# Moving the wait for the output store from SyncE into the gathering instruction of the closing barrier

## The chip, the cores and the metric

The kernel runs on one core of a Trainium2 chip. Its time is the device time of one execution in microseconds, and a run gives one such time, with a trace of the same execution. The span is the time between the first and the last record of the program in the trace; the timed execution is some 1.8 us longer than the span (1271.76 against 1270.0 us for the profiled execution before), and in the trace no instruction has a record in those 1.8 us.

The store is called "landed" when its semaphore takes its last step, and its "flight" is the time from its issue until then. In this document "tail" means: from the last step of the output store's semaphore to the end of the span. It is read from the trace's own records, which are in ns; the views print tenths of a microsecond.

## The reference

Attention over a cache for one new token, mixed with a small dense block by a gate. Cut to what matters:

```python
def reference(A_x, A_k_cache, A_v_cache, A_wq, A_wo, B_x, B_w1, B_b1, B_w2, B_b2, gate_w):
    g = _sigmoid((A_x * gate_w).sum(-1, keepdims=True))
    a = _A_ref(A_x, A_k_cache, A_v_cache, A_wq, A_wo)   # caches: 2 x 8 x 32768 x 256, bf16
    b = _B_ref(B_x, B_w1, B_b1, B_w2, B_b2)             # 448 -> 1792 -> 448
    return g * a + (1 - g) * b                          # out: 2 x 1 x 448
```

The two caches are almost all of the 547 MB that are read. The output is two rows of 448 bf16 values, 1.8 KB.

## The kernel before

Each engine has its own program inside one block. SyncE issues the loads and, at the end, the store. VectorE and ScalarE each write half of the output tile and step the semaphore `mix`; SyncE waits for both, issues the store and waits until it has landed.

```python
        def prog_sp(E):
            ...                                    # all loads
            E.wait_total("mix")
            dma(lambda e: e.dma_start(out[:, 0, :], out_sb), "d_out", "out")
            E.wait_total("d_out")                  # the store has landed
        ...
        with nc.Block("main") as block:
            ...
            block.gpsimd(lambda eng: run("pool", eng))
            block.sync(lambda eng: run("sp", eng))
            block.tensor(lambda eng: run("pe", eng))
            block.scalar(lambda eng: run("act", eng))
            block.vector(lambda eng: run("dve", eng))
```

The block closes with a barrier over the five engines: each of four reports to GpSimd, which gathers the reports and then releases all. `gather` and `release` are the two semaphores of that barrier. In the program as it is built, each engine first branches into a last block, which holds:

```text
ScalarE, TensorE, VectorE, SyncE, each:   Drain            wait: release = 0, update: gather + 1   (the report)
                                          EventSemaphore   wait: release >= 1, update: release - 1     (the take)
GpSimd:                                   Drain
                                          EventSemaphore   wait: gather >= 4, update: gather - 4       (the gather)
                                          EventSemaphore   update: release + 4                         (the release)
```

The semaphores stand on these instructions in the trace's records too; in the kernel before, `gather` takes its four steps 24, 382, 441 and 1752 ns after the start of the last cast, and the gather starts at 1776.

A wait is written as an instruction of its own, and the built program can carry it on the instruction that follows: in the trace SyncE's wait for the store stands on its branch into the last block, a record of 33 ns that starts 16 ns after the store's last step.

## Time and profile before

| | before |
|---|---|
| timed, median of the first 3 runs | 1271.65 us (1271.5 to 1271.76) |
| span of the profiled execution | 1270.0 us |
| last cast ends | 1268.38 us |
| store: issue starts, issue ends, semaphore's last step | 1268.403, 1268.732, 1269.558 us |
| tail | 1269.955 - 1269.558 = 0.397 us |

Read it from the top: the bulk is the loading of the caches (431 GB/s over the span, the DMA engines 90% busy or more in 39 of 40 slices), and no part of the change touches it. What the change can move is in the last line. The prediction shows the lines of each view.

### The profile page before, as it was taken

Reading aid. Unit: us, or ns where it says so; the run is one execution under the profiler, and the core shown is the slowest. Engines: PE = TensorE matmul, PEld = TensorE weight load, DVE = VectorE, ACT = ScalarE, POOL = GpSimd, SP = SyncE. Lnnn points to the kernel's source line nnn. Section 1 sums busy time; section 2 is a strip of 40 time slices with the busy share of each in tenths; the row PEclk is TensorE's granted clock in tenths of the full one; section 3 lists DMA queues with packets and bytes.
Section 4 is the critical chain, followed back from the end, with each engine's and each line's share of the span. In section 5 each row is a group of like instructions: output and inputs, shape, how many; then the busy total and the mean of one; then the engine's idle time right before and its main releaser. Section 6 shows DMA issues by size and latency. Waiting matters only on the chain.

```text
span 1270.0 us, 7459 instructions
## 1 busy us (share of the span) xinstructions
PE 698.5 (55%) x4386; PEld 140.6 (11%) x1842; DVE 689.9 (54%) x311; ACT 44.8 (4%) x184; POOL 4.4 (0%) x19
## 2 busy tenths in 40 slices
PE   0976456644466454565545666444764446655455
PEld 0211011100011110111001111000110001111012
DVE  4575536655365563556735466453665636557351
ACT  0100000000000000000000000000000000000000
POOL 1000000000000000000000000000000000000000
PEclk9877788777788777877768887678877778877787
DMA  9999999999999999999999999999999999999998
GB/s 408 450 429 430 430 431 436 442 431 430 429 431 438 431 438 438 431 431 429 431 438 431 436 440 431 429 431 431 440 429 436 440 431 429 431 431 440 429 425 369
DMA packets 11114, 547.58 MB, mean 431 GB/s; under 512 B 1368, under 2 KB 1632, under 8 KB 2144
## 3 DMA queue, kind: packets, MB, share of 16 engines
q1 hardware_dynamic: 10948, 547.43, 99.7%
q8 instruction: 7, 0.11, 0.0%
q10 hardware_dynamic: 156, 0.01, 0.0%
q14 instruction: 3, 0.02, 0.0%
HBM read 547.43 MB, written 0.00 MB: 431 GB/s over the span
## 4 chain that ended last, share of the span: by engine, by line
DMA 58%; PE 20%; DVE 15%; issue 5%; another core or an unknown queue 2%; ACT 0%; ACTq 0%; SPq 0%; DVEq 0%
DMA ring<-in_A_k_cache_dram 54%; DVE ring L760 12%; PE ps_s L527 7%; PE ps_s L342 6%; PE ps_o L342 4%; DMA ring<-in_A_v_cache_dram 3%; PE ps_o L576 1%; DMA PT<-in_gate_w_dram 1%; DVE mx L764 1%; PE ps_m L541 0%; PE ps_m L536 0%; PE ps_f L588 0%; DVE gmax L766 0%; PE ps_o L470 0%
## 5 line engine op out<-in xcount | busy, mean ns | idle before, releaser
L760 DVE STREAM_TRANSPOSE ring<-ring 128x4096 uint32<-128x4096 uint32 x128 | 557.6, 4413 | 385.0 <-DMA ring<-in_A_k_cache_dram 384.7
L527 PE MATMUL ps_s<-ring,Abd 128*128 128x512 bf16 x1024 | 427.9, 418 | 399.7 <-DVE ring L760 399.2
L342 PE MATMUL ps_s<-ring,Abd 128*128 128x512 bf16 x1024 | 424.4, 414 | 0.0
L527 PEld LDWEIGHTS ps_s<-ring,Abd 128*128 128x128 bf16 x1024 | 106.2, 104 | 822.1 <-DVE ring L760 456.6
L342 PE MATMUL ps_o<-ring,PT 128*24 128x512 bf16 x1504 | 112.0, 405 | 0.0
L546 PE MATMUL ps_f<-o_sb,selg 128*32 128x257 f32 x32 | 17.0, 635 | 91.1 <-DVE o_sb L793 89.9
L576 PE MATMUL ps_o<-ring,PT 128*24 128x512 bf16 x544 | 56.6, 415 | 14.3 <-DMA ring<-in_A_v_cache_dram 14.3
L764 DVE TENSOR_REDUCE mx<-ps_s 128x1 f32<-128x1024 f32 x16 | 19.6, 1225 | 60.8 <-PE ps_s L342 60.8
L677 ACT ACTIVATE negm<-ps_m 128x1 f32<-128x1 f32 x16 | 2.7, 171 | 1133.7 <-PE ps_m L541 1133.7
L777 DVE STREAM_TRANSPOSE PT<-pexp 128x1024 bf16<-128x1024 bf16 x16 | 19.9, 1245 | 36.7 <-PE ps_o L342 36.7
L793 DVE TENSOR_REDUCE o_sb<-ps_o 128x256 f32<-128x2048 f32 x15 | 34.4, 2291 | 0.5
L791 DVE TENSOR_TENSOR ps_o<-ps_o,mask 128x2048 f32<-128x2048 f32 x15 | 34.3, 2290 | 0.0
L576 PEld LDWEIGHTS ps_o<-ring,PT 128*24 128x24 bf16 x544 | 14.5, 98 | 103.9 <-issue 85.2
L774 DVE COPY ls<-lsum 128x1 f32<-128x1 f32 x16 | 2.5, 154 | 32.0 <-ACT pexp L681 32.0
L671 ACT COPY Abd<-qrep 32x16 bf16 (+1 forms) x128 | 19.5, 199 | 0.6
L681 ACT ACTIVATE pexp<-ps_s,negm 128x1024 bf16<-128x1024 f32 x16 | 17.8, 1114 | 1.7
L536 PE MATMUL ps_m<-ident_f,mx 128*1 128x128 f32 x32 | 6.1, 271 | 21.1 <-DVE mx L764 21.1
L441 PE MATMUL ps_o<-ring,xT 128*32 128x512 bf16 x16 | 5.0, 501 | 20.4 <-issue 20.4
L546 PEld LDWEIGHTS ps_f<-o_sb,selg 128*32 128x32 f32 x32 | 2.9, 140 | 109.2 <-DVE o_sb L793 107.1
L541 PE MATMUL ps_m<-ones_f,gmx 1*128 1x1 f32 x32 | 6.3, 262 | 9.9 <-DVE gmx L770 9.9
L807 DVE TENSOR_SCALAR o_sb<-ps_o,mask 128x256 f32<-128x256 f32 x1 | 0.5, 484 | 17.0 <-PE ps_o L342 17.0
L766 DVE TENSOR_REDUCE gmax<-ps_m 1x2 f32<-1x128 f32 x16 | 4.5, 278 | 7.5 <-PE ps_m L536 7.5
(87 smaller groups left out, 75.3 us busy)
## 6 DMA issues: line engine op xcount, KB each, us to landing
ring<-in_A_v_cache_dram SPq DMA_DIRECT2D x1, 4096.0 KB, 27.2
ring<-in_A_v_cache_dram SPq DMA_DIRECT2D x2, 2048.0 KB, 34.0
ring<-in_A_wq_dram SPq DMA_DIRECT2D x1, 3072.0 KB, 28.5
ring<-in_B_w_dram SPq DMA_DIRECT2D x1, 1568.0 KB, 34.5
ring<-in_A_wo_dram SPq DMA_DIRECT2D x1, 1568.0 KB, 37.9
ring<-in_B_w_dram SPq DMA_DIRECT2D x1, 1344.0 KB, 32.2
ring<-in_A_wo_dram SPq DMA_DIRECT2D x1, 1008.0 KB, 39.8
ring<-in_A_wo_dram SPq DMA_DIRECT2D x1, 560.0 KB, 40.7
```

The source lines that it names most:

```text
L342: return e.add_instruction(mybir.InstMatmult(name=f"I-{nc.next_id()}", engine=mybir.EngineType.PE, ldweights=False, ins=[e.lower_ap(x), e. ...
L527: fn = lambda e, o=o, x=x, st=st, sp=sp, s=s, w=w: e.matmul(o, a_win(s, w), x, start=st, stop=sp, skip_group_check=True)
L541: E.ins(lambda e: e.matmul(ps_m[:, C_BC:C_BC + 1], gmx[:, :], ones_f[0:1, 0:1], start=True, stop=True), key=("M2", g))
L546: E.ins(lambda e: e.matmul(ps_oa, selg[:, :], o_sb[:, :], start=False, stop=False, skip_group_check=True), key=("OT", g))
L576: fn = lambda e, o=o, x=x, wt=wt, st=st, sp=sp, j=j: e.matmul(o, wt, x, start=st, stop=sp, skip_group_check=True)
L671: E.ins(lambda e, o=o, Q=Q, c=c: e.copy(o[:, :, c:c + 2], qrep[32 * Q:32 * Q + 32, :, bass.ds(E.dyn(2 * g, 2), 2)]), key=(("A", g) if (Q = ...
L681: E.ins(lambda e: e.activation(pexp[:, :].rearrange("p (r i a) -> p i r a", r=CR, i=2), ps_s[:, :].rearrange("p (i r a) -> p i r a", i=2, ...
L760: E.ins(lambda e: e.transpose(k_words(idx, blk), k_words(idx, blk)), key=("T", idx, blk))
L764: E.ins(lambda e: e.tensor_reduce(mx[:, :], ps_s[:, :], AX.X, ALU.max), key=("MX", g))
L777: E.ins(lambda e: e.transpose(PT[:, :], pexp[:, :]), key=("PT", g))
L791: E.ins(lambda e: e.tensor_tensor(p, p, mb, ALU.mult), key=("OM", g))
L793: E.ins(lambda e: e.tensor_reduce(o_sb[:, 0:Dh], ps_o[:, :].rearrange("p (n d) -> p d n", d=Dh), AX.X, ALU.add), key=("OS", g))
```

## The change

The intent: SyncE walks through its branch and its drain, and reports to the barrier, while the store is still under way; only the gather waits for the store.

```diff
             E.wait_total("mix")
             dma(lambda e: e.dma_start(out[:, 0, :], out_sb), "d_out", "out")
-            E.wait_total("d_out")
-
         def prog_pe(E):
...
             block.vector(lambda eng: run("dve", eng))
 
 
+        done = nc.main_func.blocks[-1]
+        n0 = len(done.instructions)
+        engs["pool"].eng = nc.gpsimd
+        engs["pool"].wait_total("d_out")
+        ins = done.instructions
+        at = next(i for i, x in enumerate(ins) if x.engine == mybir.EngineType.Pool and type(x).__name__ == "InstEventSemaphore")
+        done.instructions = ins[:at] + ins[n0:] + ins[at:n0]
```

The added lines append GpSimd's wait to the last block and move it directly ahead of the gather.

## The prediction

About 0.19 us off, 1271.65 - 0.19 = 1271.46, put down as 1271.45 us.

> **What bounds the kernel now.** I read the page from the whole to the end: first the slices, then the chain that ended last, then the timeline of the last two microseconds, then the wait lists of SyncE and the view of the line that closes the block, because the change touches nothing ahead of the last store. The first view says what the bulk of the time is.
>
> ```profile
> span 1270.0 us, 7459 instructions
> ...
> DMA  9999999999999999999999999999999999999998
> ...
> HBM read 547.43 MB, written 0.00 MB: 431 GB/s over the span
> ```
>
> The 16 DMA engines are 90% busy or more in 39 of 40 slices and read the two caches at 431 GB/s. The bulk is set by what is loaded, and no load, buffer or release of a buffer is in the diff. So only the tail after the last load can change. The chain of waits, asked for its last stretch, and the timeline show it.
>
> ```profile
> 1263.41 4.57 PE ps_f L588 x62
> 1267.97 0.02 issue
> 1268.00 0.38 DVE pexp L846
> ```
>
> ```profile
> 1268.00 0.34 ACT L697 CAST pexp<-ps_f 2x224 bf16<-2x224 f32 x1 [45.80 <-PE ps_f L588]
> 1268.00 0.38 DVE L846 CAST pexp<-ps_f 2x224 bf16<-2x224 f32 x1 [7.03 <-PE ps_f L588]
> 1268.40 0.33 SPq L413 DMA_DIRECT2D out_dram<-pexp  x1
> ```
>
> The columns are start and length in us. The reader is to see that the chain view stops at the last cast (1268.00 + 0.38 = 1268.38), 1.6 us ahead of the end of the span: the store and the closing barrier are sequencer work, which it doesn't show. They are in SyncE's wait list (us in total, times, longest) and in the view of the block's last line (duration in ns, then first and last start in us).
>
> ```profile
> SPq L866 <- DMA out_dram<-pexp: 0.8, 1, 0.8
> ...
> SPq L866 <- PEq L866: 0.2, 1, 0.2
> ```
>
> ```profile
> L866 POOLq EVENT_SEMAPHORE  x2: 17/17/17, 1269.8 to 1269.8; - x2
> L866 POOLq DRAIN  x1: 529/529/529, 4.8 to 4.8; - x1
> L866 PEldq DRAIN  x1: 437/437/437, 1267.6 to 1267.6; - x1
> L866 ACTq DRAIN  x1: 368/368/368, 1268.0 to 1268.0; - x1
> L866 DVEq DRAIN  x1: 418/418/418, 1268.0 to 1268.0; - x1
> L866 SPq COMPARE_BRANCH  x1: 33/33/33, 1269.6 to 1269.6; - x1
> L866 SPq DRAIN  x1: 7/7/7, 1269.7 to 1269.7; - x1
> L866 SPq EVENT_SEMAPHORE  x1: 17/17/17, 1269.9 to 1269.9; - x1
> ```
>
> The views round to 0.1 us, so I took the same records from the trace itself, in ns after 1269 us: the store's semaphore takes its last step at 558; SyncE's branch, on which the compiled program put the wait for the store, starts at 574; SyncE's drain, which reports to the barrier, at 739; GpSimd's gather, which waits for four reports, at 772; GpSimd's release at 850; SyncE, ScalarE, VectorE and TensorE take the release at 892 to 904, and the last ends at 955, which is the end of the span. The other three reported long before: their drains end at 1268.01 (TensorE), 1268.37 (ScalarE) and 1268.43 us (VectorE). So SyncE is the last to arrive, and it arrives late because it waits for the store first and walks through a branch and a drain afterwards.
>
> [...] the branch lasts 33 ns though SyncE stood 0.8 us before it, and its start lies 16 ns after the semaphore's last step. [...] three steps, at 1268.845, 1269.526 and 1269.558 us, for a store of two rows; a waiter on GpSimd has to wait for the third just as SyncE does. [...] Here the store takes 1269.558 - 1268.403 = 1.155 us from the start of its issue to its last step, 0.826 us of it after the issue has ended (1268.732)[...].
>
> **The change part by part.**
> - Removed: SyncE's wait for the store ahead of its branch. It is no instruction of its own in this trace, so none disappears. What it did was to hold the branch until 1269.574 us.
> - Moved: SyncE's branch and drain. They start right after the issue. From the wait's end, the drain started 739 - 574 = 165 ns after the branch, and the gather 33 ns after the drain. With the issue ending at 1268.732, I expect the branch near 1268.75, the drain near 1268.92 and the report visible near 1268.95 us. That is some 0.6 us before the store lands, all of it under the store's flight.
> - Added: the wait for the store, on GpSimd. It is placed directly before the gather. In this trace two pure waits in a row on TensorE appear as one EVENT_SEMAPHORE with two wait terms (three such records, 51 ns each, like its single ones), so I expect GpSimd's gather to become one instruction with two waits, still 17 ns long, rather than a new instruction. I choose that as the main case; the other is a rival below.
> - The new end: the gather now waits for the store alone, since four reports are in by 1268.95. After a DMA's last step SyncE took 16 ns to start; by the trace's records VectorE took 23 to 24 ns in every one of its waits that ended with a cache tile's last landing, and TensorE 28 to 29 ns in those where a sequencer instruction waited. I take 16 to 28 ns for GpSimd, so the gather starts at 558 + 16 to 558 + 28 = 574 to 586 instead of 772: earlier by 186 to 198 ns. Everything after it (78 ns to the release, 42 to 54 ns to the four takers, 51 ns for the last) stays.
> - Sum: about 0.19 us off a span of 1270.0 us, which is 0.015%. On the timed median: 1271.65 - 0.19 = 1271.46, predicted as 1271.45 us.
>
> **The rivals.**
> 1. The wait stays an instruction of its own on GpSimd. Then it starts at about 580, and the gather follows one step later. The only pair of semaphore instructions in a row on GpSimd here is gather and release, 78 ns apart at both barriers (607 and 686 ns after the start of the span; 772 and 850 at the end). The gain shrinks to 772 - (580 + 78) = 0.11 us: 1271.54 us. The word "in" of the change's description speaks against it, as do TensorE's double waits.
> 2. A drain that waits for transfers takes the removed wait's place: SyncE's drain would hold until the store has landed, and the report would come no earlier than now. Gain 0 to 0.16 us, time 1271.5 to 1271.65 us. Against it speaks the opening barrier of the same trace: SyncE issues the first cache tile, 8 MB, at 0.0 us and its drain there runs from 0.46 to 0.58 us, while VectorE can start on that tile only at 21.94 us. A drain does not wait for landing.
> 3. The saving is real in the span and vanishes from the timed number. The timed execution of the profile is 1271.76 us against a span of 1270.0 us, so 1.8 us lie outside of what is recorded. If that part waits on something else that runs beside the barrier, the time stays 1271.65 us. Nothing in the profile speaks for or against it.
> 4. The bulk moves by itself. The three runs before span 1271.76 - 1271.50 = 0.26 us, more than the gain[...]. The program's layout hardly changes, so I expect no shift with a cause, only scatter.
>
> **Range and chances.** The rivals span 1271.46 to 1271.65 us, so the range is set by scatter and not by them. Three runs of one load of the program say little about another load, so I widen their 0.26 us to about 0.85 us on either side: 1270.6 to 1272.3 us. 2% of the time is 25 us, fifteen times all that happens after the last cast (1.6 us), so neither faster nor slower by over 2% can come from the change; I leave 1% each for a disturbed run. Within 2%: 98%.
>
> **What would show each step right or wrong.** In the changed kernel's view of the closing line, SyncE's drain should start near 1268.9 on this trace's scale, ahead of the store's last step, instead of after it; if it starts after landing, rival 2 holds. GpSimd should have two EVENT_SEMAPHORE records there, not three; three would be rival 1. In the wait lists, SyncE's 0.8 us on the store should be gone, and its wait for the barrier should grow from 0.2 to about 1.0 us. From the store's last step to the span's end should be about 0.20 us instead of 0.397 (1269.955 - 1269.558). If that distance shrinks and the timed median doesn't follow, it is rival 3 or 4, and only many rounds on one chip can tell them apart. The prediction is wrong if GpSimd answers a DMA's semaphore much later than the 16 to 28 ns seen on the other engines: no wait of GpSimd on a DMA exists in this trace to check it.

## The result

| | before | changed |
|---|---|---|
| timed, median of 6 runs | 1271.7 us (1271.5 to 1272.03) | 1271.47 us (1271.41 to 1271.55) |
| ratio of the fast runs | | 0.9998, interval 0.9985 to 1.0011 |
| span of the profiled execution | 1270.0 us | 1269.6 us |
| tail | 0.397 us | 0.196 us |

A ratio is the mean time of one kernel's fast runs over that of the other's of the same rounds, so not quite the ratio of the medians that are quoted. 0.2 us of 1270 us is far inside the interval. The slowest of the changed kernel's six runs (1271.55) is slower than the fastest of the six before (1271.5), so the two sets of timed numbers overlap and do not settle a gain of this size by themselves. The trace does.

First the bulk, from the windows view of the stretch from 240 to 1240 us (busy us of TensorE, its weight loads, VectorE, ScalarE and GpSimd, then granted clock, DMA share, GB/s). Before:

```profile
240.00:1240.00 1000.00, 547.12 (x3442) 104.25 (x1333) 543.23 (x221) 31.32 (x135) 0.00 (x0) 0.77 1.00 433
```

Changed:

```profile
240.00:1240.00 1000.00, 545.33 (x3448) 103.83 (x1332) 543.12 (x221) 31.28 (x135) 0.00 (x0) 0.77 1.00 433
```

The same 433 GB/s and the same work: the bulk did not change. The profile's span fell by 0.345 us by the records (1269.955 to 1269.610). Of that, 0.140 us is the last cast, which starts at 1267.856 instead of 1267.996 us; over the fourteen traces it starts anywhere between 1267.86 and 1268.07, whatever the kernel, so this part is scatter. The rest is behind the cast. The timeline of the changed kernel shows its end (start and length in us):

```profile
1267.86 0.38 DVE L844 CAST pexp<-ps_f 2x224 bf16<-2x224 f32 x1 [6.93 <-PE ps_f L586]
1268.26 0.33 SPq L413 DMA_DIRECT2D out_dram<-pexp  x1
```

The store is issued 0.41 us after the cast started, as before. The view of the block's last line (now L864: the change took two lines out above it), with durations in ns and first and last start in us:

```profile
L864 POOLq EVENT_SEMAPHORE  x2: 17/314/612, 1268.8 to 1269.5; - x2
...
L864 SPq DRAIN  x1: 143/143/143, 1268.7 to 1268.7; - x1
L864 SPq EVENT_SEMAPHORE  x1: 17/17/17, 1269.5 to 1269.5; - x1
```

SyncE's wait list of the changed kernel:

```profile
SPq L864 <- PEq L864: 0.8, 1, 0.8
```

SyncE's branch has no record any more, its drain has moved from 1269.7 to 1268.7 us, ahead of the landing, and its wait for the store is gone from the list; the time is in its wait for the barrier. GpSimd still has two records on that line, but the gather is now 612 ns long instead of 17.

By the trace's records, in ns after the start of the last cast:

| | before | changed |
|---|---|---|
| store's issue ends | 736 | 736 |
| SyncE's branch, drain | 1578, 1743 | no record, 807 |
| store's semaphore, last step | 1562 | 1558 |
| gather starts, ends | 1776, 1793 | 976, 1588 |
| release starts | 1854 | 1650 |
| end of the span | 1959 | 1754 |

The gather ended 231 ns after landing before and 30 ns after it now: 201 ns saved. All the rest of the tail kept its length (61 ns and then 105 ns before, 62 and 104 ns now).

### The profile page after: what moved, and what is told of

Its sections match the earlier page's. It is cut to its first block, busy times and chain, and to the rows that moved or that the text cites. A ratio compares the mean times of both kernels' runs of the same rounds, so it can differ in the third digit from the quotient of the medians.

```text
span 1269.6 us, 7458 instructions
## 1 busy us (share of the span) xinstructions
PE 699.4 (55%) x4386; PEld 141.0 (11%) x1842; DVE 690.0 (54%) x311; ACT 44.7 (4%) x184; POOL 4.4 (0%) x19
## 4 chain that ended last, share of the span: by engine, by line
DMA 61%; PE 19%; DVE 14%; issue 5%; SPq 0%; ACT 0%; ACTq 0%
DMA ring<-in_A_k_cache_dram 57%; DVE ring L758 12%; PE ps_s L525 6%; PE ps_s L342 6%; PE ps_o L342 4%; DMA ring<-in_A_wo_dram 3%; DVE mx L762 1%; DMA PT<-in_gate_w_dram 1%; PE ps_o L574 1%; PE ps_m L539 0%; PE ps_m L534 0%; DVE gmax L764 0%; PE ps_o L468 0%; DVE gmx L768 0%; PE ps_o L439 0%
## 5 line engine op out<-in xcount | busy, mean ns | idle before, releaser
L342 PE MATMUL ps_o<-ring,PT 128*24 128x512 bf16 x1504 | 114.0, 411 | 0.0
L574 PE MATMUL ps_o<-ring,PT 128*24 128x512 bf16 x544 | 57.9, 424 | 12.8 <-DMA ring<-in_A_v_cache_dram 12.8
```

The source lines that it names most:

```text
L342: return e.add_instruction(mybir.InstMatmult(name=f"I-{nc.next_id()}", engine=mybir.EngineType.PE, ldweights=False, ins=[e.lower_ap(x), e. ...
L574: fn = lambda e, o=o, x=x, wt=wt, st=st, sp=sp, j=j: e.matmul(o, wt, x, start=st, stop=sp, skip_group_check=True)
```

## The experiments

The theory: what counts is the chain of steps that stands behind the landing of the store, whoever waits. The rivals: the engine that waits decides; the gain is a shift of the bulk; SyncE's own work at the end is overlapped anyway. Twelve kernels were run, each with five rounds, all correct. The runs came in four calls (null to sp_drain; release to drains6_before; the other three with drains; all_take). A call's runs share one chip, and each call has nine runs of the kernel before as its yardstick. "Timed" below is the mean of the kernel's runs less the mean of the runs of before in the same call.

| run | tail, ns | change of the tail, us | timed, us | timed less span, us |
|---|---|---|---|---|
| null | 397 | 0 | -0.06 | 1.81 |
| again | 196 | -0.20 | -0.25 | 1.80 |
| pool_own | 299 | -0.10 | -0.18 | 1.82 |
| sp_drain | 288 | -0.11 | -0.15 | 1.84 |
| release | 128 | -0.27 | -0.31 | 1.82 |
| sp_take | 23 | -0.37 | -0.83 | 1.42 |
| pool_branch | 440 | +0.04 | -0.02 | 1.82 |
| drains6_before | 557 | +0.16 | +0.08 | 1.83 |
| drains6_after | 196 | -0.20 | -0.30 | 1.83 |
| drains24_after | 879 | +0.48 | +0.43 | 1.80 |
| drains24_before | 1486 | +1.09 | +0.94 | 1.85 |
| all_take | 41 | -0.36 | -0.38 | 1.87 |

The last column is the mean over the runs of the timed number less the span of the same execution; for the kernel before it is 1.83, 1.83, 1.81 and 1.85 us in the four calls. The timed differences follow the tail to within 0.15 us, and they carry a lean of some -0.06 us, as the null run shows. One run stands out, sp_take.

### The kernel before against itself (null)

Edit: a comment at the end of the file.

> The kernel before against itself: shows the scatter that a gain of 0.2 us has to stand against. Both theories: store's last semaphore step to the end of the span 397 ns as in the first trace, timed medians within 0.15 us of each other, ratio 1.0000 within 0.0002.

Measured: tail 397 ns; five runs from 1271.67 to 1271.85 us against nine from 1271.64 to 1271.97 us; ratio 0.9999. As expected. A timed difference below about 0.1 us says nothing here.

### The changed kernel once more (again)

Edit: a comment at the end of the changed kernel.

> The changed kernel once more. Theory (SyncE's branch, drain and report have moved under the store's flight): last step to end 196 ns, 0.20 us less than the kernel before, and the timed mean 0.15 to 0.25 us lower. Rival (the timed 0.23 us of the first result is a shift between loads or of the bulk): the distance is 196 ns, but the timed difference is anything between -0.3 and +0.3 us.

Measured: tail 196 ns; timed -0.25 us against before, and 1271.56 - 1271.75 = -0.19 us against the null run, all five runs of which (1271.67 and up) lie above all five of this one (1271.66 and down). Of the nine runs of before one (1271.64) is faster than this one's slowest. The gain is there on a second load and another set of rounds, which makes a shift between loads unlikely as its only cause; that the timed numbers follow the tail through all but one of the runs below speaks more strongly against it.

### GpSimd waits in an instruction of its own (pool_own)

```diff
         engs["pool"].eng = nc.gpsimd
+        engs["pool"].wait_total("mix")
         engs["pool"].wait_total("d_out")
```

The added wait is long satisfied. In the built program it takes the place in the gather (the trace's record of the gather has `gather` and `mix`), so that the wait for the store stays an instruction of its own ahead of it.

> GpSimd waits for the store in an instruction of its own directly before the gather. If an instruction of its own is a step of some 78 ns as between gather and release: last step to end 16 + 78 + 78 + 105 = 277 ns, gain over the kernel before 0.12 us. If it is free [...]: 196 ns, gain 0.20 us.

Measured: tail 299 ns. The own wait starts 24 ns after landing, the gather 66 ns after that, and the gather, with two waits that are both satisfied, lasts 43 ns instead of 17. So an instruction of its own costs 299 - 196 = 103 ns here, and half the gain is lost with it. The expected 277 ns were 22 ns short: the gather is 26 ns longer and the answer 8 ns later (24 for 16), and the step to the gather is 12 ns shorter (66 for 78).

### SyncE waits behind its branch (sp_drain)

```diff
-        engs["pool"].eng = nc.gpsimd
-        engs["pool"].wait_total("d_out")
+        engs["sp"].eng = nc.sync
+        engs["sp"].wait_total("d_out")
         ins = done.instructions
-        at = next(... x.engine == mybir.EngineType.Pool and type(x).__name__ == "InstEventSemaphore")
+        at = next(... x.engine == mybir.EngineType.SP and type(x).__name__ == "InstDrain")
```

> SyncE still waits for the store, but behind its branch and before its drain. Theory: only the branch moves under the store's flight; an own wait (16 ns after landing), one step of some 78 ns to the drain, 33 ns to the gather, 78 to the release, 105 to the end: 310 ns, gain over the kernel before 0.09 us. Rival (any move of the wait off SyncE's program gives the whole gain, or the engine that waits decides): 196 ns or 397 ns.

Measured: tail 288 ns, timed -0.15 us. SyncE still waits itself and more than half of the gain is there: 109 of 201 ns. From the wait to the drain it now takes 55 ns, where from the branch to the drain it took 165; the difference, 110 ns, is the gain. (The expectation took 78 ns for that step, hence 310 ns.) Both rivals fall: neither the whole gain nor none.

### GpSimd waits ahead of its own branch (pool_branch)

```diff
+            E.wait_total("d_out")        # last line of GpSimd's program in the main block
...
-        done = nc.main_func.blocks[-1]   # and the six lines after it
```

> GpSimd waits for the store, but ahead of its own branch into the closing block, as SyncE did in the kernel before. Theory (what counts is the steps behind the wait, not which engine waits): branch 16 ns after landing, 165 ns to the drain, a step of 60 to 80 ns to the gather, 78 to the release, 105 to the end: about 430 ns, no gain, or up to 0.05 us slower than the kernel before. Rival (SyncE is slow at waiting for its own store and GpSimd is not): about 196 ns, a gain of 0.20 us.

The view of the block's last line (L865 in this kernel):

```profile
L865 POOLq EVENT_SEMAPHORE  x2: 17/17/17, 1269.8 to 1269.9; - x2
...
L865 SPq DRAIN  x1: 143/143/143, 1268.8 to 1268.8; - x1
L865 POOLq COMPARE_BRANCH  x1: 33/33/33, 1269.6 to 1269.6; - x1
L865 POOLq DRAIN  x1: 41/41/41, 1269.7 to 1269.7; - x1
```

Measured: tail 440 ns, timed -0.02 us. SyncE's drain is as early as in the changed kernel, and nothing is gained: the branch that carries the wait is now GpSimd's, with its 33 ns and 149 ns from its start to the drain (1586 to 1735). So moving the wait to another engine does nothing by itself; what is left to walk through behind it counts.

### GpSimd waits in the release (release)

```diff
-        at = next(i for i, x in enumerate(ins) if x.engine == mybir.EngineType.Pool and ... "InstEventSemaphore")
+        at = [i for i, x in enumerate(ins) if x.engine == mybir.EngineType.Pool and ... "InstEventSemaphore"][1]
```

> GpSimd waits for the store one instruction later than in the change: in the release, after the gather. Theory (only what stands behind the landed store on the longest path counts): the gather and its step to the release move under the flight too; the release starts 16 to 30 ns after landing and the end follows 104 ns later: last step to end 120 to 134 ns, 0.27 us under the kernel before, 0.07 us under the changed one. Rival (GpSimd's turn after a wait has a fixed cost of some 196 ns to the end): 196 ns, as the changed kernel.

Measured: tail 128 ns, timed -0.31 us. The gather runs at 976 ns after the cast with its old 17 ns, and the release starts 24 ns after landing. One more step has moved under the store's flight, worth 196 - 128 = 68 ns in the trace. The two were not timed in one call, so the timed numbers do not settle 0.07 us.

### SyncE waits in its last instruction (sp_take)

```diff
-        engs["pool"].eng = nc.gpsimd
-        engs["pool"].wait_total("d_out")
+        engs["sp"].eng = nc.sync
+        engs["sp"].wait_total("d_out")
         ins = done.instructions
-        at = next(... x.engine == mybir.EngineType.Pool and type(x).__name__ == "InstEventSemaphore")
+        at = next(... x.engine == mybir.EngineType.SP and type(x).__name__ == "InstEventSemaphore")
```

> SyncE waits for the store in its very last instruction, the one that takes the release, so the whole barrier runs under the store's flight. Theory: last step to end 17 to 35 ns, 0.37 us under the kernel before in the span. If the timed execution follows the span, its mean is 0.3 to 0.4 us lower; rival (the part of the timed execution outside the span starts when the other engines are through, or waits on something else): the span falls by 0.37 us and the timed mean by less than 0.25 us.

The view of the block's last line:

```profile
L864 POOLq EVENT_SEMAPHORE  x2: 17/17/17, 1268.9 to 1269.0; - x2
...
L864 SPq EVENT_SEMAPHORE  x1: 491/491/491, 1269.0 to 1269.0; - x1
L864 ACTq EVENT_SEMAPHORE  x1: 17/17/17, 1269.0 to 1269.0; - x1
L864 PEldq EVENT_SEMAPHORE  x1: 51/51/51, 1269.0 to 1269.0; - x1
L864 DVEq EVENT_SEMAPHORE  x1: 21/21/21, 1269.0 to 1269.0; - x1
```

The whole barrier is over at 1269.0 us and SyncE alone stays, 491 ns, until the store has landed. Tail 23 ns, as expected. But the timed mean is 0.83 us lower (five runs from 1270.81 to 1271.13, nine of before from 1271.66 to 1272.05), twice what the span gives: the part outside the span has shrunk from 1.83 to 1.42 us. No theory had this. The last engine besides SyncE ends its part at 1158 ns after the cast here and at 1959 in the kernel before, 0.80 us earlier. That suggests that the timed number follows those engines and that SyncE's later end is covered by what comes after; the next run tests it.

### All five engines wait at their end (all_take)

```diff
+        for nm, e, typ in (("sp", nc.sync, "SP"), ("pe", nc.tensor, "PE"), ("act", nc.scalar, "Activation"),
+                           ("dve", nc.vector, "DVE"), ("pool", nc.gpsimd, None)):
+            ...                              # the wait, folded into the take; GpSimd's own one behind its release
```

> All five engines wait for the store in their last instruction of the block, GpSimd in one of its own behind the release. It is there because with SyncE alone waiting there, the part of the timed execution outside the span fell from 1.83 to 1.42 us, which no theory had. Both theories: last step to end 30 to 75 ns, the span some 0.33 to 0.37 us under the kernel before. Theory A (the four engines let go early run the unrecorded ending work ahead, under the store's flight): held together again, the part outside the span is back at 1.80 to 1.85 us and the timed mean 0.3 to 0.4 us under the kernel before. Theory B (the barrier's own instructions being behind the store, or SyncE's last instruction, shortens what comes after): 1.42 us outside again, timed 0.75 us or more under.

The view of the block's last line:

```profile
L864 SPq EVENT_SEMAPHORE  x1: 491/491/491, 1269.0 to 1269.0; - x1
L864 ACTq EVENT_SEMAPHORE  x1: 491/491/491, 1269.0 to 1269.0; - x1
L864 DVEq EVENT_SEMAPHORE  x1: 492/492/492, 1269.0 to 1269.0; - x1
L864 PEldq EVENT_SEMAPHORE  x1: 491/491/491, 1269.0 to 1269.0; - x1
```

Measured: tail 41 ns, timed -0.38 us, outside the span 1.87 us (1.85 for the kernel before). SyncE's last instruction is the same as in sp_take, and the barrier runs as early; only the other four are held until the landing. The additional 0.4 us are gone. So theory A stands: they came from the engines that were let go early, and theory B falls. What those engines do in the unrecorded part, which of the four sets the time, and whether SyncE's own part is what limits sp_take at 1.42 us, stays open.

### Six and 24 drains on SyncE, with the wait before and after the change

```diff
             dma(lambda e: e.dma_start(out[:, 0, :], out_sb), "d_out", "out")
             E.wait_total("d_out")            # in the two "before" kernels only
+            for _ in range(6):               # or 24
+                E.ins(lambda e: e.drain(), key=None)
```

> The kernel before with six bare drains on SyncE behind its wait for the store: an amplifier. Theory: all of it stands behind landing; a step of some 57 ns each (from wait to drain in the earlier run with the wait ahead of the drain), so last step to end 397 + 6 x 57 = about 740 ns, 0.34 us above the kernel before. Rival (SyncE's sequencer work at the end is overlapped in any case): 397 ns.

> The changed kernel with the same six drains on SyncE directly behind the store's issue. In the changed kernel the gather has its four reports 587 ns before the store lands. Theory: six drains at some 57 ns, 340 ns, fit under that: last step to end 196 ns, the same as the changed kernel without them, 0.2 us under the kernel before. Rival (the gather is held by SyncE's report after all): some 540 ns.

> The changed kernel with 24 drains on SyncE behind the store's issue: more than fits. Theory: 24 x 57 = 1370 ns against a slack of 587 ns, so the report comes some 780 ns after landing and the end some 980 ns after it; timed some 0.6 us above the kernel before. It measures how much of SyncE's work the store's flight can hide. Rival (slack of another size, since drains may wait for the store's own work): the distance tells the slack.

> The kernel before with 24 drains on SyncE behind its wait. Theory: last step to end 397 + 24 x 57 = about 1765 ns, timed 1.37 us above the kernel before. Against the changed kernel with as many drains the gain of the move is then capped by the flight of the store, some 0.79 us (587 + 201 ns), and is large enough for the timed numbers to show it well.

The view of the drains' line, with shortest, median and longest ns and first and last start, in the changed kernel with 24 drains:

```profile
L415 SPq DRAIN  x24: 7/7/143, 1268.8 to 1270.2; - x24
```

and in the kernel before with 24:

```profile
L416 SPq DRAIN  x24: 7/7/7, 1269.5 to 1270.7; - x24
```

Measured tails: 557 and 1486 ns with the wait ahead of the drains, 196 and 879 ns with the wait in the gather. With six drains the changed kernel's tail is the same 196 ns as without: they are hidden whole. Ahead of the barrier they cost 557 - 397 = 160 ns. With 24, more than the flight can hide, the move is worth 1486 - 879 = 607 ns in the trace and 1272.73 - 1272.22 = 0.51 us timed, where the two kernels' runs no longer touch (1272.66 and up, 1272.34 and down). So the rival "SyncE's work at the end is overlapped in any case" falls, and so does "the gather is held by SyncE's report".

The expected sizes were off (740, 980 and 1765 ns for 557, 879 and 1486), for reasons that the records show. A drain follows the last one after 52 ns and not 57. With drains behind the wait, the wait rides on the first drain and no longer on the branch, and the step across the branch takes 55 ns (1850 to 1905) instead of 165: from the wait to the closing drain it is 325 ns with six drains against 165 with none. And behind the store's issue the first drain lasts 143 ns and the next starts 200 ns after it, against 63 ns when it stands behind the landed store; so the move lets SyncE start 774 ns earlier (806 instead of 1580), loses 137 ns of that at the first drain and 26 ns at the gather, which takes 43 ns with two satisfied waits instead of 17: 611 ns, 607 with the 4 ns by which the landings differ. I had expected 785.

## Why the prediction was right

The time, 1271.47 us, lies 0.02 us from the predicted 1271.45 us, inside the range, and "within 2%" held. That it is so near is luck: the six runs of before alone lie up to 0.53 us apart. The tail is the test: 0.196 us for a predicted "about 0.20". By the prediction's own steps:

- **What bounds the kernel.** Right: the bulk is the same to the digit in GB/s, and its scatter (0.2 us in the start of the last cast over fourteen traces) is as large as the gain.
- **Removed: the wait that held the branch.** Right, and sp_drain and drains6_before show more than the step claimed: of the 201 ns, 110 are the branch being the instruction that waits.
- **Moved: SyncE's branch and drain.** The report came as early as predicted: the gather's first wait was satisfied at 976 ns after the cast, 1268.97 us on the scale of the trace before, for "near 1268.95". The way there was different: the drain started 71 ns after the issue's end, earlier than predicted, and lasted 143 ns instead of 7. That the two misses cancel is luck. The opening barrier that the prediction uses against its second rival had already shown a drain of 121 ns behind an issue.
- **Added: one gather with two waits.** Right that it is one instruction; wrong that its record stays 17 ns long. It is 612 ns, from the reports being in to 30 ns after the store has landed. The ground given for 17 ns was misread: of the three double waits of TensorE in the trace before, two are 51 ns long, but the third is 20,601 ns long (10.067 to 30.668 us) and ends 34 ns after the last step of its second semaphore. It already shows what the gather's record then did.
- **The new end.** Predicted 186 to 198 ns earlier, measured 201: the gather was to end 33 to 45 ns after landing (16 to 28 and its own 17) and ends 30 ns after it. GpSimd's answer to a DMA's semaphore, which no wait of the trace before could show, takes 24 ns in pool_own, pool_branch and release, inside the 16 to 28 taken from the other engines.
- **Rival 1, a wait of its own**, was named as a gain of 0.11 us; pool_own measured 98 ns in the tail. It did not occur in the change.
- **Rival 2, a drain that waits for the landing**: no. The drain behind the issue lasts 143 ns and ends at 950 ns after the cast, 608 ns ahead of the landing. That it lasts 143 ns and not 7 is hidden under the flight; why it lasts longer is not shown.
- **Rival 3, the timed number does not follow the span**: not in the change (1.82 us outside the span, 1.83 before). sp_take shows that the number outside can move, but to the better.
- **Rival 4, scatter**: it is of the size of the gain, as said; the null run leans by 0.06 us.
- **SyncE's wait for the barrier** was to grow to about 1.0 us and is 0.8.

The kernels that go further beat the changed one in the trace: release by 68 ns in the tail, all_take by 155 ns, and sp_take, the fastest kernel at 1270.93 us median, by 173 ns. SyncE's own program still doesn't end before the store has landed in sp_take, and its result was correct. It lets the other four engines leave before that; this is the last block of the program, and beyond the correct result nothing was tested about what may follow it.

## What to carry to other kernels

Find who arrives last at a barrier and what it still has to walk through after its last wait; a wait is best placed in the latest instruction that still must not run early, so that everything before it passes while the transfer is under way: here the tail was 397 ns with the wait on SyncE's branch, 288 with it behind that branch and ahead of SyncE's drain, 196 in the gather, 128 in the release and 23 in SyncE's own last instruction. A wait that rides on a branch was dear here (165 ns to the next instruction on SyncE and 149 on GpSimd, against 55 from SyncE's wait behind the branch), so put it elsewhere. And weigh such a move by the trace: 0.2 us of 1270 us is real and all but invisible to the timed number.

## What else the records show

- With two waits in one instruction, the record began when the one that the trace lists first was satisfied: the gather's record is 612 ns in the change, and SyncE's take 491 ns in sp_take, both ending 23 to 30 ns after the store landed. In drains24_after the second one, the store, was satisfied first, 670 ns before the gather's record began, and that record is only 43 ns long: in these three records the place in the list decided, not which came first in time. With one wait, the release in the run of that name begins 24 ns after landing and is 17 ns long.
- Two satisfied waits make the gather 43 ns long instead of 17 (pool_own, drains24_after). On TensorE two of the trace's double waits are 51 ns long, as its single ones are.
- A branch on which a wait is put, unconditional in the built program, is a COMPARE_BRANCH of 33 ns here, with the next instruction 165 ns (SyncE, before) or 149 ns (GpSimd, pool_branch) after its start; without a wait it leaves no record, and the step across it is 55 ns (drains6_before), 3 ns more than between two drains.
- A drain directly behind an issue takes 143 ns behind the store's (7 ns behind the landed store) and 121 ns in the opening barrier. The one behind the store's ends about 100 ns after the first of the three steps of the store's semaphore (950 and 848 ns after the cast, in the change).
